# A two-layer strided convolution with a joint network: the first tap in two column parts, its load halves between the sample blocks, and every engine's order as a table

## The chip, the core and the metric

The kernel runs on one core of a Trainium2 chip. The metric is the device time of one execution, in microseconds (us). A core has five engines that each work through a queue of their own: TensorE (PE in the profile; its weight loads are PEld), VectorE (DVE), ScalarE (ACT), GpSimd (POOL) and SyncE (SP), which here only issues DMAs.

## What is computed

```python
def reference(x, w1, w2, g, w_f, w_g, w_o):      # x: (2, 4000, 512), w1, w2: (5, 512, 512), g: (2, 8, 512)
    pad = K // 2
    xp = jnp.pad(x, ((0,0),(pad,pad),(0,0)))
    h = sum over i of einsum("btc,cd->btd", xp[:, i:i+T, :], w1[i])
    h = _gelu(h)[:, ::2, :]
    ...
    f = _gelu(the same with hp and w2)[:, ::2, :]
    fe = jnp.einsum("btd,de->bte", f, w_f)
    ge = jnp.einsum("bud,de->bue", g, w_g)
    j = jnp.tanh(fe[:, :, None, :] + ge[:, None, :, :])
    return jnp.einsum("btud,dv->btuv", j, w_o)
```

Two convolutions of five taps over time, each followed by gelu and by keeping every second row, then for each of 2 x 8 pairs a tanh of a sum and a last product with w_o. All data is bf16; the output is (2, 1000, 8, 512).

## The kernel before

Everything lies transposed, channels in the 128 partitions (four blocks of 128 channels, k = 0 to 3), time along the columns. The program is first written down as a list of operations (class `Plan`), each with its engine, its reads and writes and a cost; `edges` finds what must wait for what, `schedule` sets the order of every engine, and `emit` writes the queues and semaphores. An operation made with `flex` may go to either of two engines, and `schedule` settles which.

The work comes in these stages.

- **Start.** A memset, eight products of zeros on PE (`warm_mm`), the loads on SP. The first 218 x 4 samples of batch 0 come as two blocks `xr[0]` (128 rows) and `xr[1]` (90 rows), each row four samples long. PE turns each block in two operations (even and odd sample phases, `pp` = 0 and 1) of eight transposes each, into PSUM banks 4 to 7; DVE copies the two results of the first block into `xs[0]` (line 527), ACT those of the second (line 525).
- **Direct products.** `direct(i, m)` multiplies tap i of w1, output block m, with columns of `xs[0]`: for the first 216 outputs of batch 0, two neighbouring outputs side by side (2 x 216 = 432 columns), four channel blocks each, into banks 0 to 3. The taps go in the order 0, 4, 2, 1, 3. Taps 0, 4 and 2 read even phases (2 and 0), taps 1 and 3 odd ones. Four ACT operations (line 712) apply gelu and write `hT[0]`.
- **Triples.** The rest of both layers goes by a scheme that makes three outputs from fewer products: `Triple` forms sums and differences of the samples (`step`, on DVE and ACT: "d", "r", "t2", "tm", "sm", "t1", "s1", ...), `w1part` and `w2part` form sums of the taps (on DVE and ACT, into `w1_t`, `w1_x`, `w2_t`), and `Unit` issues the products of one output block in five parts s1 to s5. The first two triples have 262 columns, the others 334.
- **Joint part.** `fe` and `ge`, then tanh on ACT into `jT` and `jX`, then the last product. It goes in blocks of four tiles by a scheme with seven products instead of eight (`Seven`: `sums` form operand sums, on POOL or DVE by `flex`; p1 to p7 are the products, whose results ACT or DVE evict and add), and some plain tiles (`Plain`). SP stores the tiles.

What sets the order around the change. On SP the order before is: `xr[0]`, `xr[1]`, tap 0 of w1 in two column halves (256 of 512 columns each, all four channel blocks), then taps 4, 2, 1, 3 whole, then twelve transposing loads into `xq`, six into `xp[2]`, and the rest. `load_w1` lets each whole tap wait for an earlier load (`o.after.append(came[-3].idx)`): tap 4 for `xr[0]`, tap 2 for `xr[1]`, tap 1 for tap 0, tap 3 for tap 4. In `schedule` a time line is played through with the costs; PE takes the earliest operation that is ready, SP and POOL by index, ACT and DVE by the latest time at which an operation may end, all but PE corrected by one letter for each operation in the string `NUDGES`. Operations made while `pl.pin` is set (all up to the gelu of the direct part) keep their order on their engine.

Of the kernel before, what the change touches and what calls it, by code (L numbers as in the profile page):

```python
# [12 lines left out]
P = 128  # L13
# [37 lines left out]
class Psum:  # L51
# [6 lines left out]
    def pair(self, lo, step, n):  # L58
        ap = self.h[:, lo:lo + 2 * step].rearrange("p (s c) -> p s c", s=2)[:, :, 0:n]
# [9 lines left out]
NUDGES = (  # L69
    "WWWWWWWWWWWWWWWWWWWWWWWWWWWWWWWWWWWWWWWWWWWWWWWWWWWWWWWWWWWWWWWWWWWWWWWWWWWWWWWZGRxV4s1q-S-zIwUDlPB1btjPJVWAWWfYOS-0KT0d"  # L70
    "dIkA-0yl2ZWWWWWWWWWWWyWWQEqWWMWWm8ddCa1B0-yn00WoWW2KtWW7WWPWWg8HCWeWW1mZWWDWW0WWakaF--VX-W0WWOrTWWXWWUWW5WwWWJ-4WW_WW-WW"
    "-5T00vmWGWW70RWW6WW-WWb-mtW4WWGlgWW0WW0WW6-a2YwvXTWiWWKSvWWsWWaWW0W-WW-n-WWcWW_WWjsHUAloWWWWWW5Jd-Pq-WBWWD-2WW4WWeWWw-S0"
    "0fmDvt3RUh-W-WWY--WW-WWAWWEX4iYejb0992kFIky15WNWW2tUWW6WWkWWfuUox0NRL-GW-WW_S8WWSWW4WW0-z4Oe-ByzWdWWh-eWWrWWXWWnLu0W0WWi"
    "8-WWHWWKWWBJ0VxX26uWSWWf1RWW-WWPWWTW-WWtS4WW1WWjWW9WWWW-Zk-d0WYWWq-pWWOWWWWWcO-AWNWW0pSWWQWWzWWPqIYZ---bW4WWi06WW-WW-WWl"
    "WWWWyWW46MD-WW7_0WlW0MW-W-eWZWwnW0Wb0WW_WWXWhWfWWrW-i0-S2VEu4WWsWWbWW0WW9qj9BWWqWW-WWWMe0z0WWoWWKWWWWW4WWsy092WWSWWWWWWL"
    "WWWWWZWW-WW-WWnWWSW0O-SrWWaWWZWWWHWWW8rzw6WWxWW-WWDWWkWWOwFlY6-WWPWWIWWWhWWWWWuoeb4WWYWWYWWiWWqWW7H3IDWWGWWIWWWsWW-n2WWy"
    "WWRWW0WW_WW9W4tRWWCWWLWWWEWWWWW00-X-WWpWWUWWxWWQWWjcm7aWW0WWqWWW-WWWGqTWWoWW-WWlWW-WFQ7DiWWEWWVWWW-WWWW00-g_sjWWUWW0WW-W"
    "W-WyN---WW-WW3WWWTWWc0zz-WWHWWwWWGWWsWp9TM-WWzWWLWWW0WWWyfWWDWW2WWAWWQWE7E0kWW-WWjWWW0WduWW0WWAWW4WWUWpxUpFWWlWW3WWWdWWW"
    "WWwWWOWWJWWLWlzPsiWWzWWoWWWyWg0EOWWqWWAWWqWW9E9XdWWNWW0WWWIWWWNG0-yKWWsWW8WWEWWbI0LPWW-WW6WWW0W1yWW8WWTWWhWWsI_qTWWqWWQW"
    "WWPWWWwBWW-WWrWW-WWpYyqiWWDWWZWWWUW49WW7WWdWWFWWp5_FFWWQWWWWWW6WWWdXE0WWLWWAWWrWW07LstWWWWWtWWWsWxEBY8cWW3WW1WWwWWOVPnsW"  # L80
    "W0WWJWWWOWWWGEWW0WWYWW-WWHCX_fWWmWWCWWW0WC4WWVWWFWWJWW0W-WW-j0WWrWWaWWWWW5WZ-WWfWWFWW1WWOWqW--rmWW5WWdWWWJWWWG-lSWWTWWPW"
    "WbWW0Rrw1WW-WWqWWWDWeXsFWW0WWpWWfWW82Id5WWkWWPWWW8WWW6EWWiWWYWWMWW7W1tSWWdWWkWWWeWx2WW3WW-WWMWWSUx45WWyWWYWWWFWWWWW3WWyW"
    "W-WWfWxWD-qzWW0WWJWWWcWWWTWWtWWrWWyWNWWWWzWWJWWW1WWUWW3WWXWWWhWW0WLWWiW")


class Plan:
# [88 lines left out]
    def schedule(self, pred):  # L175


        ops, HOP = self.ops, self.HOP
        n = len(ops)
        succ = [[] for _ in ops]  # L180
        for i, p in enumerate(pred):
            for j in p:
                succ[j].append(i)
        span = [o.cost + (4.0 if o.dma else 0.0) for o in ops]
        late, nextpe = [0.0] * n, 0.0
        for i in range(n - 1, -1, -1):
            t = min([late[s] - (HOP if pred[s][i] else ops[i].cost - span[i]) for s in succ[i]], default=0.0)
            if ops[i].eng == "pe":
                t = min(t, nextpe)
            late[i] = t - span[i]  # L190
            if ops[i].eng == "pe":
                nextpe = late[i]
        nudge = [0.1 * (ALPHABET.index(c) - 32) for c in NUDGES] if len(NUDGES) == n else [0.0] * n
        left = [len(p) for p in pred]
        ready = [0.0] * n
        free = {e: 0.75 for e in ("pe", "act", "dve", "pool", "sp")}
        cand = {e: [] for e in free}

        def engines(i):
            return ops[i].alt or (ops[i].eng,)  # L200

        for i in range(n):
            if not left[i]:
                for e in engines(i):
                    cand[e].append(i)
        order = {e: [] for e in free}
        wire, lock, start = 0.0, 0.0, [0.0] * n
        for _ in range(n):
            best = None
            for e, c in cand.items():  # L210
                if c:
                    t = max(free[e], min(ready[i] for i in c))
                    if best is None or t < best[0]:
                        best = (t, e)
            t, e = best
            now = [i for i in cand[e] if ready[i] <= t + 0.02]
            i = min(now, key=(lambda i: i) if e == "pe" else (lambda i: (0.15 * i + nudge[i], i)) if e in ("sp", "pool") else (lambda i: (late[i] + nudge[i], i)))
            for f in engines(i):
                cand[f].remove(i)
            order[e].append(i)  # L220
            o = ops[i]
            if o.alt:
                o.eng, (o.fn, o.cost), o.alt = e, o.alt[e], None
            start[i] = t
            free[e] = t + o.cost
            if o.port:
                if lock > t - 0.2 and e == "dve":
                    free[e] = max(t, lock) + o.cost + 0.2
                elif lock > t:
                    free[e] = lock + o.cost  # L230
                lock = free[e]
            end = free[e]
            if o.dma:
                wire = max(wire, t + 1.8) + o.wire
                end = max(wire, t + 2.0)
            for s in succ[i]:
                ready[s] = max(ready[s], end + HOP if pred[s][i] else free[e])
                left[s] -= 1
                if not left[s]:
                    for f in engines(s):  # L240
                        cand[f].append(s)
        self.start = start
        self.end = max(free.values())
        return order

    def emit(self, block, tail):
        nc, ops = self.nc, self.ops
        pred = self.edges()
        order = self.schedule(pred)
# [71 lines left out]
def bass_standalone__seq2seq_rnn_t_joint__speech_kernel(  # L321
# [25 lines left out]
    NA, N3 = 216, 262  # L347
# [9 lines left out]
    with ExitStack() as es:  # L357
# [33 lines left out]
        xq = [Buf(nc, f"xq{i}", [6, NK, 288], BF16, v.end - v.bytes) for i, v in enumerate((xs[1], w2_sb))]  # L391
# [85 lines left out]
        came = [load_xr(rt) for rt in range(2)]  # L477
        act(warm[0:1], warm[1:2], ACT.Gelu_apprx_tanh)

        def load_w1(i):  # L480
            src = w1[i].rearrange("(k c) d -> c k d", c=P)
            if len(came) == 2:
                h = D // 2
                for sl in (slice(0, h), slice(h, D)):
                    o = pl.dma("sp", lambda e, sl=sl: e.dma_start(w1_sb[i, :, sl].ap, src[:, :, sl]), (), (w1_sb[i, :, sl],), nbytes=262144)
            else:
                o = load_w("sp", w1_sb[i], src)
                o.after.append(came[-3].idx)
            came.append(o)

        def load_xq(i, ph):
            load_x6(xq[i], 0, ph, 2 * NA // 3 + i * N3 - 2, 0, -(-(N3 + 3 - i) // 16) * 16)

        for kind, i in (('w', 0), ('w', 4), ('w', 2), ('w', 1), ('w', 3), ('x', 4), ('x', 0), ('x', 2), ('x', 1), ('x', 3), ('x', 5)):
            if kind == "w":
                load_w1(i)
            else:
                load_xq(0, i)
        for ph in (4, 0, 2, 1, 3, 5):
            load_xq(1, ph)  # L500
# [8 lines left out]

        warm_mm(NWARM)  # L510
        psb = ps.h[:, :].bitcast(BF16)
        for rt in range(2):
            for pp in range(2):
                bk, n = 4 + 2 * pp + rt, NR[rt]
                pv = View(psb[:, bk * 1024:(bk + 1) * 1024].rearrange("p (r k c) -> p r k c", r=2, k=NK)[:, :, :, 0:n], np.array([bk]), True)

                def fn(e, rt=rt, pp=pp, pv=pv, n=n):
                    for r in range(2):
                        for k in range(NK):
                            ins = e.transpose(pv.ap[:, r, k, :], xr[rt].h[0:n, 2 * r + pp, k, :], ident.h[0:n, 0:n])  # L520
                    return ins
                pl.op("pe", fn, (xr[rt].rows(0, n), ident[:]), (pv,), 0.55)
                o = xs[0][pp::2, :, 16 + rt * P:16 + rt * P + n]
                if rt:
                    act(o, pv, ACT.Copy)
                else:
                    pl.op("dve", lambda e, o=o, pv=pv: e.tensor_copy(out=o.ap, in_=pv.ap), (pv,), (o,), vec_cost(o, (pv,)))
# [158 lines left out]
        for b in range(B):  # L686
            memset(hT[b][4:6, :, HOFF - 1:HOFF])
            memset(hT[b][:, :, HOFF + NT3:HOFF + NT3 + 2])
# [17 lines left out]
        for i in taps:  # L706
            for m in range(NK):
                direct(i, m)
# [437 lines left out]
```

## Time and profile before

| | us |
|---|---|
| median of 3 runs | 252.21 (251.29 to 252.4) |
| profiled execution | 252.07 |
| its span in the profile | 250.3 |
| around the span | 1.77 |
| PE busy in the span | 245.5 |
| DVE, ACT, POOL busy | 207.8, 209.9, 106.7 |
| first direct product starts | 7.29 |
| last product's result evicted by ACT from | 247.42 |

The clock granted to PE in the profiled execution is 1.00 of full speed. The profile gives the span of one execution, engine by engine. A line of the timeline gives start, duration, engine, source line, operation, the tile written and the tiles read, shapes and how many instructions are merged; in brackets the idle time before and what ended it. A busy time of PE is that of overlapping products and tells little of its pace; the distance between starts does.

### The profile page before, as it was taken

Reading aid. Unit: us, or ns where it says so; the run is one execution under the profiler, and the core shown is the slowest. Engines: PE = TensorE matmul, PEld = TensorE weight load, DVE = VectorE, ACT = ScalarE, POOL = GpSimd, SP = SyncE. Lnnn points to the kernel's source line nnn. Section 1 sums busy time; section 2 is a strip of 40 time slices with the busy share of each in tenths; the row PEclk is TensorE's granted clock in tenths of the full one; section 3 lists DMA queues with packets and bytes.
Section 4 is the critical chain, followed back from the end, with each engine's and each line's share of the span. In section 5 each row is a group of like instructions: output and inputs, shape, how many; then the busy total and the mean of one; then the engine's idle time right before and its main releaser. Section 6 shows DMA issues by size and latency. Waiting matters only on the chain.

```text
span 250.3 us, 5204 instructions
## 1 busy us (share of the span) xinstructions
PE 245.5 (98%) x1920; PEld 184.5 (74%) x1920; DVE 207.8 (83%) x346; ACT 209.9 (84%) x354; POOL 106.7 (43%) x109
## 2 busy tenths in 40 slices
PE   8999999999999999999999999999999999999995
PEld 4556888887666666667467878877778888888873
DVE  1599999968999997981528978899899999999763
ACT  2297799978969868963699998999999999999673
POOL 1000000000000000002429898598998999998910
PEclk9999999999999999999999999999999999999999
DMA  7999999988500052000002223422344444564547
GB/s 212 307 187 173 192 164 212 147 173 262 163 0 3 0 169 85 1 1 3 0 0 84 86 84 105 151 88 84 112 145 131 160 154 141 171 211 156 185 162 240
DMA packets 57392, 31.92 MB, mean 128 GB/s; under 512 B 33837, under 2 KB 57149, under 8 KB 57367
## 3 DMA queue, kind: packets, MB, share of 16 engines
q1 hardware_dynamic: 57367, 31.59, 48.2%
q8 instruction: 15, 0.25, 0.4%
q14 instruction: 10, 0.08, 0.1%
HBM read 7.71 MB, written 16.38 MB: 96 GB/s over the span
## 4 chain that ended last, share of the span: by engine, by line
PE 89%; DVE 4%; DMA 4%; ACT 1%; issue 1%; DVEq 0%
PE acc L442 89%; DMA w_sb<-in_w_dram 2%; DMA xr<-in_x_dram 1%; DVE ssum L429 1%; DVE ssum L530 1%; DVE w_t L429 1%; DVE row L429 1%; ACT hT L434 1%; ACT w_x L434 0%; ACT ost L434 0%; DVE w_x L429 0%; ACT sd L434 0%; DVEq L282 0%
## 5 line engine op out<-in xcount | busy, mean ns | idle before, releaser
L429 DVE TENSOR_TENSOR og<-acc,sn 128x512 bf16<-128x512 f32 x87 | 56.7, 680 | 5.4 <-PE acc L442 4.7
L434 ACT ACTIVATE jT<-feT,geT 128x1000 bf16<-128x1000 f32 (+6 forms) x56 | 51.3, 961 | 0.5 <-DVE feT L755 0.4
L442 PE MATMUL acc<-tw,ss 128*128 128x256 f16 x348 | 48.3, 273 | 0.0
L442 PEld LDWEIGHTS acc<-tw,ss 128*128 128x128 f16 x348 | 33.7, 98 | 7.0 <-issue 0.4
L931 POOL TENSOR_TENSOR ss<-jT 128x512 f16<-128x512 bf16 x26 | 31.4, 1218 | 11.8 <-ACT jT L434 9.2
L442 PE MATMUL acc<-row,w_sb 128*128 128x334 bf16 (+1 forms) x192 | 33.1, 295 | 0.0
L862 ACT ACTIVATE sn<-acc 128x512 f32<-128x512 f32 x51 | 30.6, 619 | 2.6 <-PE acc L442 2.3
L442 PE MATMUL acc<-wo_sb,jT 128*128 128x256 bf16 (+1 forms) x196 | 31.6, 288 | 0.0
L426 POOL MEMSET hT<- 128x8 bf16 (+2 forms) x6 | 0.7, 149 | 71.6 <-ACT hT L434 66.7
L442 PE MATMUL acc<-row,w_x 128*128 128x262 bf16 (+1 forms) x192 | 28.5, 290 | 0.2 <-ACT sd L434 0.2
L434 ACT ACTIVATE jX<-feT,geT 128x1000 bf16<-128x1000 f32 (+4 forms) x28 | 25.0, 919 | 0.0
L442 PEld LDWEIGHTS acc<-row,w_sb 128*128 128x128 bf16 x192 | 18.5, 98 | 6.7 <-DVE acc L530 0.3
L442 PEld LDWEIGHTS acc<-row,w_x 128*128 128x128 bf16 x192 | 18.6, 98 | 6.1 <-ACT sd L434 0.5
L442 PEld LDWEIGHTS acc<-wo_sb,jT 128*128 128x128 bf16 x196 | 19.1, 98 | 5.3
L434 ACT ACTIVATE sd<-acc 128x334 f32<-128x334 f32 (+1 forms) x48 | 20.3, 429 | 2.6 <-PE acc L442 2.1
L530 DVE SCALAR_TENSOR_TENSOR acc<-acc,sd 128x334 f32<-128x334 f32 (+1 forms) x24 | 11.6, 482 | 11.4 <-PE acc L442 11.4
L434 ACT ACTIVATE hT<-acc 128x262 bf16<-128x262 f32 (+2 forms) x36 | 15.4, 433 | 6.7 <-PE acc L442 6.6
L863 DVE COPY sn<-acc 128x512 f32<-128x512 f32 x26 | 17.6, 682 | 3.9 <-PE acc L442 3.9
L931 POOL TENSOR_TENSOR ss<-jX 128x512 f16<-128x512 bf16 x17 | 20.3, 1209 | 1.2 <-ACT jX L434 0.7
L931 POOL TENSOR_TENSOR ss<-jT,ss 128x512 f16<-128x512 bf16 x15 | 17.8, 1191 | 1.0 <-DVE ss L931 0.7
L442 PE MATMUL acc<-wo_sb,ss 128*128 128x256 bf16 x116 | 17.7, 273 | 0.0
L931 POOL TENSOR_TENSOR ss<-ss,jT 128x512 f16<-128x512 f16 x15 | 17.5, 1173 | 0.6 <-DVE ss L931 0.4
(105 smaller groups left out, 499.7 us busy)
## 6 DMA issues: line engine op xcount, KB each, us to landing
out_dram<-og SPq DMA_DIRECT2D x44, 256.0 KB, 2.2
w_sb<-in_w_dram SPq DMA_DIRECT2D x9, 512.0 KB, 5.1
out_dram<-og SPq DMA_DIRECT2D x14, 128.0 KB, 2.2
out_dram<-ost SPq DMA_DIRECT2D x7, 128.0 KB, 2.0
xr<-in_x_dram SPq DMA_DIRECT2D x1, 512.0 KB, 3.4
w_sb<-in_w_dram SPq DMA_DIRECT2D x2, 256.0 KB, 5.3
wf_sb<-in_w_f_dram SPq DMA_DIRECT2D x1, 512.0 KB, 3.7
wg_sb<-in_w_g_dram SPq DMA_DIRECT2D x1, 512.0 KB, 4.7
```

Of the source, the lines that this page charges most:

```text
L426: pl.op("pool", lambda e: e.memset(v.ap, 0.0), (), (v,))
L429: pl.op(eng, lambda e: e.tensor_tensor(out=o.ap, in0=a.ap, in1=b.ap, op=op), (a, b), (o,), 0.02 + 2.14e-3 * o.ap.free_size() if eng == "po ...
L434: pl.op("act", lambda e: e.activation(o.ap, i.ap, func, scale=scale, bias=0.0 if bias is None else bias.ap), rd, (o,), o.ap.free_size() * ...
L442: ins = e.matmul(o.ap, lhsT=l.ap, rhs=r.ap, start=start and n == 0, stop=stop and n == len(pairs) - 1, skip_group_check=not check)
L530: pl.op(eng, lambda e: e.scalar_tensor_tensor(out=o.ap, in0=a.ap, scalar=f, in1=b.ap, op0=ALU.mult, op1=add), (a, b), (o,), vec_cost(o, (a ...
L862: pl.flex({"act": (lambda e: e.activation(o.ap, v.ap, ACT.Copy), 0.05 + n * 0.833e-3), "dve": (lambda e: e.tensor_copy(out=o.ap, in_=v.ap) ...
L863: "dve": (lambda e: e.tensor_copy(out=o.ap, in_=v.ap), 0.065 + n * 1.04e-3)}, (v,), (o,))
L931: fn = lambda e, o=S[i], x=x, y=y, op=op: e.tensor_tensor(out=o.ap, in0=x.ap, in1=y.ap, op=op)
```

## The change

1. **Loads.** Tap 0 of w1 is loaded in halves by channel block (k = 0, 1 and k = 2, 3, all 512 columns) instead of by output column. The order on SP becomes `xr[0]`, first half, `xr[1]`, second half, tap 4, 2, 1, 3. Tap 4 waits for no earlier load any more; tap 2 waits for `xr[1]`, tap 1 for tap 0's second half, tap 3 for tap 4.
2. **Tap 0 in two column parts.** The outputs 0 to 127 of each of the two halves (2 x 128 = 256 columns) need only the first block; they are multiplied first, for k = 0, 1 and then for k = 2, 3. Then the outputs 128 to 215 (2 x 88 = 176 columns). Instead of 16 products of 432 columns there are 16 of 256 and 16 of 176.
3. **The second block's turn** goes behind the first eight products of tap 0.
4. **Copies.** Of each block, DVE copies the even phases and ACT the odd ones.
5. **Order.** `schedule` no longer plans: `ORDER` gives the indices of all 1643 operations (12 more than before) engine by engine, two letters for each. For `flex` operations the table settles the engine, too. DVE has 369 operations (346 before), ACT 343 (353), POOL 92 (105), SP 142 (142), PE 697 (685). SP's order behind the first eight loads is the one of before.
6. `N3` becomes a pair with the same two values, and the width of `xq` is worked out from it to the same 288. `pair` writes its access pattern so that the second part may lie across the end of the first pair. The memsets of `hT` and `xq` change place in the list.

```diff
+ORDER = {
+    "pe": (
+        "0X0Y0Z0a0b0c0d0e0f0h0l0m0n0o0p0r0t0u0v0w0x0y0z0_0-101112131415161718191A1B1C1D1E1F1G2O1s1H1I352o1u1v2V2W2Q2R2q2y2z2r"
...
+    def schedule(self):
+
+        order = {k: [64 * ALPHABET.index(a) + ALPHABET.index(b) for a, b in zip(s[::2], s[1::2])] for k, s in ORDER.items()}
+        assert sorted(i for v in order.values() for i in v) == list(range(len(self.ops)))
+        for k, v in order.items():
+            for i in v:
+                o = self.ops[i]
+                if o.alt:
+                    o.eng, (o.fn, o.cost), o.alt = k, o.alt[k], None
...
-        came = [load_xr(rt) for rt in range(2)]
+        def load_w1(i, parts=1, ks=(0,)):
+            n = NK // parts
+            for k in ks:
+                src = w1[i, k * P:(k + n) * P].rearrange("(k c) d -> c k d", c=P)
+                dst = w1_sb[i, k:k + n]
+                o = pl.dma("sp", lambda e, dst=dst, src=src: e.dma_start(dst.ap, src), (), (dst,), nbytes=n * 131072)
+                if len(came) > 4:
+                    o.after.append(came[-3].idx)
+                came.append(o)
+
+        came = [load_xr(0)]
+        load_w1(0, 2, (0,))
+        came.append(load_xr(1))
+        load_w1(0, 2, (2,))
         act(warm[0:1], warm[1:2], ACT.Gelu_apprx_tanh)
...
+        load_w1(4)
+        for i in (2, 1, 3):
+            load_w1(i)
...
         warm_mm(NWARM)
...
+        turn(0, 0, "dve")
+        turn(0, 1, "act")
...
+        for q0, n in ((0, P), (P, NA - P)):
+            for ks in ((0, 1), (2, 3)):
+                for m in range(NK):
+                    mm(ps.pair(m * NT + q0, NA, n), [(w1_sb[0, k, m * P:(m + 1) * P], both(0, k, q0, n)) for k in ks],
+                       q0 == 0 and ks[0] == 0, False, False)
+                if q0 == 0 and ks[0] == 0:
+                    turn(1, 0, "dve")
+                    turn(1, 1, "act")
+        for i in taps[1:]:
+            for m in range(NK):
+                direct(i, m)
```

`turn(rt, pp, eng)` holds the eight transposes of one block's phases and the copy of their result, as the loop at lines 512 to 527 did, with the engine of the copy as an argument.

More of the change, by code (lines that the diff above doesn't have):

```diff
@@ L58, in pair @@
     def pair(self, lo, step, n):
[L59 removed]
+        lo_ap = self.h[:, lo:lo + n]
+        ap = bass.AP(tensor=lo_ap.tensor, offset=lo_ap.offset, ap=[list(lo_ap.ap[0]), [step, 2], [1, n]])
         cells = np.unique(np.concatenate([np.arange(lo, lo + n), np.arange(lo + step, lo + step + n)]) // 512)
@@ L173, in edges @@
         return pred
[L175 to L243, printed above, removed]
@@ L247, in emit @@
         nc, ops = self.nc, self.ops
-        pred = self.edges()
-        order = self.schedule(pred)
+        order = self.schedule()
         pred = self.edges()
@@ L390, in bass_standalone__seq2seq_rnn_t_joint__speech_kernel @@
         assert all(xp[i].end <= xs[i].end for i in xp)
-        xq = [Buf(nc, f"xq{i}", [6, NK, 288], BF16, v.end - v.bytes) for i, v in enumerate((xs[1], w2_sb))]
+        XQ = [-(-(N3[i] + 3 - i) // 16) * 16 for i in range(2)]
+        xq = [Buf(nc, f"xq{i}", [6, NK, XQ[i] + 16], BF16, v.end - v.bytes) for i, v in enumerate((xs[1], w2_sb))]
         assert xq[0].end <= xs[1].end and xq[1].end <= w2_sb.end
```

137 lines of the change are left out of this document (70 added, 67 removed).

## The prediction

> **What bounds the kernel now.** I read the page's engine shares first, then the chain of work that ended last, the timeline of the first 30 us, and the busy time by stretches.
>
> ```profile
> PE 245.5 (98%) x1920; PEld 184.5 (74%) x1920; DVE 207.8 (83%) x346; ACT 209.9 (84%) x354; POOL 106.7 (43%) x109
> ```
>
> PE is busy almost throughout. A busy PE need not be at its pace, so I compared start-to-start distances of the products with the pace of their width: 0.183 us for 432 columns (80 products, 14.81 us, below), 0.112 for 262, 0.109 for 256. From the first product at 7.29 to the last, all the waits together are about 0.9 us.
>
> ```profile
> 4.58 2.17 PE L520 MATMUL acc<-ident,xr 128*128 128x128 bf16 x32
> ...
> 5.67 1.29 DVE L527 COPY xs<-acc 128x1024 bf16<-128x1024 bf16 x2 [4.54 <-PE acc L520]
> 6.46 1.44 ACT L434 ACTIVATE xs<-acc 128x720 bf16<-128x720 bf16 x2 [4.23 <-PE acc L520]
> ...
> 7.29 14.81 PE L442 MATMUL acc<-xs,w_sb 128*128 128x432 bf16 x80 [0.54 <-ACT xs L434]
> 9.77 1.29 DVE L530 SCALAR_TENSOR_TENSOR ssum<-w_sb 128x512 f32<-128x512 bf16 x2 [2.81 <-DMA w_sb<-in_w_dram]
> ...
> 21.94 1.50 PE L442 MATMUL acc<-row,w_x 128*128 128x262 bf16 x12
> ...
> 23.61 2.99 PE L442 MATMUL acc<-row,w_x 128*128 128x262 bf16 x24 [0.17 <-ACT sd L434]
> ```
>
> Columns are start, duration, engine. All 32 turns of the sample blocks come first, two copies on DVE and two on ACT follow, and the first product starts when ACT's first copy (6.46 to 7.23) is done. The waits: 21.94 + 12 x 0.112 = 23.28, but the next product starts at 23.61 (0.33); another 0.12 before 25.08; 0.10 in two small ones up to 32; and 0.36 from 34 us on, of which 0.15 at 136.9 and 0.13 at 238.5.
>
> ```profile
> 0.74 3.45 DMA xr<-in_x_dram
> 4.18 0.02 issue
> 4.20 5.55 DMA w_sb<-in_w_dram
> 9.75 0.02 issue
> 9.77 1.29 DVE ssum L530 x2
> ...
> 23.61 223.79 PE acc L442 x1788
> ```
>
> This is the chain in order of time. Before 23.61 it does not run through PE: it runs from the landing of tap 4 of w1 (9.75) through DVE, which has no pause from there:
>
> ```profile
> 9.77:23.60 13.83, 13.67 (x80) 7.54 (x78) 13.83 (x23) 10.35 (x17) 0.24 (x2) 1.00 1.02 204
> 23.60:34.00 10.40, 10.39 (x91) 8.59 (x92) 10.40 (x21) 7.90 (x17) 0.33 (x2) 1.00 1.09 188
> ...
> 125.00:180.00 55.00, 55.00 (x436) 42.27 (x435) 45.24 (x75) 54.34 (x86) 43.80 (x38) 1.00 0.27 87
> 180.00:240.00 60.00, 60.00 (x528) 50.82 (x526) 55.83 (x91) 57.23 (x93) 56.43 (x49) 1.00 0.49 159
> ```
>
> After length and sum stand PE, PEld, DVE, ACT, POOL (instructions in brackets), clock, DMA. DVE is full in both early stretches. So two things must come earlier for the end to move: PE's first product, and DVE's results.
>
> **The start.** Nothing changes until the first block is turned: it lands at 4.18, 16 transposes follow from 4.58, DVE's copy runs 5.67 to 6.36. The first piece of tap 0 needs this copy and half of w1's tap 0, which now travels second. Half a tap is 262 KB, 0.74 us at the 354 GB/s below, so it lands near 5; 1.3 us to spare. With 0.06 from a copy's end to a product (7.23 to 7.29 above), products start at 6.42 instead of 7.29: 0.87 earlier. But the second block's 16 transposes (starts 5.93 to 6.54 at 0.039 apart, 0.64 with the last) stood before 7.29 where PE would have waited anyway; now they stand between products and cost 0.64. The pieces of tap 0: 16 of 256 columns at 0.109, and 16 of 176 columns, between the 90-column (0.039) and 256-column rows, on the line through 262 and 432 columns 0.076. Together 2.96 against 16 x 0.183 = 2.93: 0.03 lost (-0.4 if free, +0.5 at the 256-column row). Net 0.87 - 0.64 - 0.03 = **0.20 earlier**. Cover: the second block landed at 5.67; 0.74 later at most is 6.4, and its transposes start at 6.42 + 8 x 0.109 = 7.29. Its DVE copy (0.5) ends near 8.3, wanted at 8.80. Tap 0's other half, at worst 7.6 as now, is wanted at 7.93.
>
> Two copies (first block's odd rows, second block's odd rows) go on ACT behind two w_x conversions that wait for DVE's chain. They run about 13.4 to 15.1 (conversions 12.30 to 13.5 now, copies 1.03 and 0.77) and are wanted by tap 1 at 6.42 + 0.64 + 2.96 + 5.86 = 15.88: hidden, 0.8 of cover. POOL now has an xp memset that waits for the last direct product (22 us) ahead of the memsets of hT and xq; their readers come after 30 us, and the xq ones wait for a load landing at 33 anyway. SP's queue keeps its order behind the start, so its stores cost nothing new.
>
> **DVE's chain.** It starts when tap 4 lands. Tap 4 no longer waits for the first block on SP (issue 4.20), but that wait hides nothing: the DMA engines are full, in rows of the stretches:
>
> ```profile
> 5.00:6.50 1.50, 1.50 (x29) 1.50 (x27) 0.83 (x2) 0.04 (x1) 0.00 (x0) 1.00 1.14 279
> 7.50:10.50 3.00, 3.00 (x18) 1.63 (x17) 0.73 (x2) 0.39 (x1) 0.00 (x0) 1.00 1.06 354
> ```
>
> The first holds tap 0's column halves (packets of 512 bytes), the second whole taps (1024 bytes). The new halves are row blocks with 1024-byte packets: 524 KB at 354 instead of 279 GB/s take 1.48 instead of 1.88 us, so all that follows, tap 4 first, lands about **0.4 earlier**: 9.35. Bounds: 0, and 1.2 (tap 4's 5.55 us behind an issue at about 3.0 is 8.55).
>
> The Trainium skill, page DMA: Bandwidth & Descriptors, section Specifications, gives 512 bytes as the least transfer for line rate; by that rule the old halves already ran at it and tap 4 would come no sooner. The two rows above disagree with it, 279 against 354, though the first stretch also holds other packets. This is the third rival below.
>
> Now DVE's new queue. In the order before, the step "t1" of the first triple, which PE's third group of products (s3) reads, is the 24th DVE instruction from 9.77 and starts at 23.71, 0.606 apiece. In the table it is the 27th: three more weight sums of later column blocks stand ahead. It starts at 9.35 + 26 x 0.606 = 25.11, and is there for PE at 25.11 + 0.70 + 0.06 = 25.87. PE reaches s3 after 6.42 + 0.64 + 2.96 + 64 x 0.183 + 32 x 0.112 = 25.31. So a new wait of **0.56** before s3 takes the place of 0.33 and 0.12; 0.10 of small ones stay. Lateness of PE at 34 us: after 6.42 + 0.64 + 0.03 + 0.56 + 0.10 = 7.75; before 7.29 + 0.33 + 0.12 + 0.10 = 7.84. The start's 0.20 comes out as **0.09**: DVE eats the rest. If tap 4 comes as now it is 0.31 worse, +0.3 in all; if it comes 1.2 earlier PE never waits and 0.7 is won.
>
> **The table behind 34 us.** Matching indices (the new program has 12 more, all in the start), 27 strided sums leave POOL for DVE and 14 go back: net 13. Net 10 evictions and copies leave ACT for DVE.
>
> ```profile
> L931 POOL TENSOR_TENSOR ss<-jT x26: 1147/1164/1397, 130.0 to 235.3; 128x512 f16<-128x512 bf16 x26
> ...
> L931 DVE TENSOR_TENSOR ss<-jT x11: 412/426/907, 125.9 to 232.8; 128x512 f16<-128x512 bf16 x11
> ...
> L931 DVE TENSOR_TENSOR ss<-ss,jT x4: 424/1313/1357, 129.4 to 164.2; 128x512 f16<-128x512 f16 x4
> ```
>
> Minimum, median, maximum in ns: a sum on DVE takes 0.42, but up to 1.36 where one on POOL is running. DVE gets 13 x 0.42 + 10 x 0.60 = 11.5 us at best, while the 30 sums already there (mean 0.70) may lose up to 30 x 0.28 = 8.4 as POOL gets 13 fewer. I wrote out the table's queues with these durations: each instruction starts when its engine and its inputs allow. No product waits over 0.1 except one: near 238.5 a p4 product needs the eviction of p7, which stands on DVE behind a sum that meets a POOL sum or just misses it: 0.43 or 0. All waits behind 34 us: 0.11 to 0.54, against 0.36 now; I take the middle, 0.33, **0.03 won** (bounds -0.25 and +0.2; below these lies only the second rival).
>
> **The sum.** 0.09 + 0.03 = 0.1 us off the profiled execution, whose time is 252.07 (span 250.3 and 1.77 around it): 251.95. The median shown is 252.21, 0.14 above; I give **251.9**. 0.5%, 1.26 us, is about what a measurement of this kernel can tell from no change.
>
> **Rivals.**
> 1. Tap 4 lands 0.8 to 1.2 earlier, as its issue is earlier and its packets need not follow the others. Then the wait before s3 is 0.2 or none, and without the wait at 238.5: 0.7 + 0.25, 251.1. For it: 2.81 us of DVE idle before 9.77; against: DMA shares over 1. Chance 0.17; a third of it lies beyond 0.5%.
> 2. Slower: DVE becomes the bound. If all sums on DVE stay at a mean of 0.70, it gets 13 x 0.70 + 10 x 0.60 = 15.1 us in the stretches 125 to 240, where it has 9.8 + 4.2 = 14.0 idle; the spare is never all usable, so +1.1 and some: 253.6. It decides from (14.0 - 6.0) / 13 = 0.62 us a sum upward. For it: 56 of 60 us busy in the second stretch; against: POOL's load falls by 13 x 1.16 = 15 us. Chance 0.10.
> 3. Packet size changes nothing and tap 4 lands at 9.75: 252.07 + 0.3 = 252.3. Chance 0.15.
> 4. The change doesn't do what it says, because a piece waits for its load, or PE's clock falls in the pause from 5.93 to 6.42. The pause of 0.7 before 7.29 now left the clock at 1.00. DVE's queue hides up to 0.56 of such a loss: 252.0 to 252.5. Chance 0.08.
>
> The forecast itself, 251.5 to 252.4, has 0.50. Faster by over 0.5% 0.07, slower by over 0.5% 0.10, the rest, 0.83, within. The range takes in rivals 1, 3 and 4 and the doubt of a median (the three times shown span 1.1): 251.0 to 252.9.
>
> **What will show it.** First product of 256 columns at 6.4 and 16 transposes of 90 behind the eighth; DVE's first weight sum at 9.35; a wait of some 0.56 before s3 near 25.9, released by DVE; ACT's two copies near 14 without a wait of PE; sums on DVE mostly at 0.42. Wrong would make it: a wait at 7.3 or 7.9 released by a load, a PE wait for ACT near 15.9, or many sums on DVE over 1 us with PE waiting behind them.

## The result and the profile after

The changed kernel takes **254.09 us** (median of 4 runs, 253.67 to 254.34) where the kernel before takes 252.12 (4 runs, 251.29 to 252.4). The ratio is 1.0085, with a 95% interval of 1.0068 to 1.0101: slower by about 2 us. The forecast was 251.9, with a range up to 252.9. The profiled execution took 254.12, with a span of 252.3 against 250.3. Two executions at a granted clock of 0.974 (265.04 of the kernel before, 266.29 in experiment 7) are in no median or ratio of this text.

The page's engine shares, first as before:

```profile
PE 245.6 (97%) x1932; PEld 186.2 (74%) x1936; DVE 212.8 (84%) x369; ACT 203.6 (81%) x344; POOL 90.0 (36%) x96
```

The work has moved as the diff says (POOL 106.7 to 90.0, ACT 209.9 to 203.6, DVE 207.8 to 212.8), and PE's is the same (the page lacks the records of four of the 1936 products that the change should show). So the 2 us are waits and a longer end. The timeline of the start:

```profile
4.57 1.91 PE L485 MATMUL acc<-ident,xr 128*128 128x128 bf16 x16
...
6.42 1.24 PE L407 MATMUL acc<-xs,w_sb 128*128 128x256 bf16 x8
...
7.50 0.81 PE L485 MATMUL acc<-ident,xr 90*128 90x90 bf16 x16
...
9.18 0.69 DVE L499 SCALAR_TENSOR_TENSOR ssum<-w_sb 128x512 f32<-128x512 bf16 x1 [0.62 <-DMA w_sb<-in_w_dram]
```

The first product starts at 6.42, as forecast, and the first weight sum at 9.18 (forecast 9.35). The chain in order of time shows where the execution then waited:

```profile
9.58 7.47 DMA xq<-in_x_dram
17.07 1.08 ACT row L399
...
24.14 0.29 ACT sd L399
24.42 0.05 issue
24.47 96.84 PE acc L407 x748
...
133.21 1.91 DVE ss L908 x2
135.12 0.61 DVE og L394
135.73 0.05 issue
135.78 83.10 PE acc L407 x700
...
248.56 0.38 ACT ost L399
```

The early part runs no longer through DVE from tap 4 on, but through the first load into `xq` and ACT. A second piece that was not there before leads through ACT and DVE to 135.78; its last steps are two sums on DVE and the `og` behind them. The stretches:

```profile
5.00:6.50 1.50, 1.50 (x15) 1.30 (x14) 0.69 (x1) 0.00 (x0) 0.00 (x0) 1.00 0.96 275
7.50:10.50 3.00, 3.00 (x44) 2.82 (x42) 1.86 (x4) 0.00 (x0) 0.00 (x0) 1.00 0.80 242
...
125.00:180.00 55.00, 53.95 (x425) 41.37 (x425) 47.21 (x87) 51.50 (x81) 35.15 (x31) 1.00 0.26 85
180.00:240.00 60.00, 59.90 (x525) 50.76 (x525) 57.45 (x102) 55.99 (x88) 50.89 (x46) 1.00 0.48 157
```

The DMA engines, full from 7.5 to 10.5 before (354 GB/s), moved 242. From 5.0 to 6.5 they moved 275, no more than the 279 of before.

To add the waits up I use PE's **lateness**: the start of a product, less what all products ahead of it take at the pace of their width (the start-to-start distances of each width, as in the prediction; a product without a record is counted in where the gap shows it). It rises only where PE waits. The last column is what follows the last product.

| us | at 9 | at 34 | at 132 | at 136.5 | at the end | to the span's end |
|---|---|---|---|---|---|---|
| before | 7.30 | 7.87 | 7.88 | 7.88 | 8.34 | 3.07 |
| after | 7.28 | 8.05 | 8.16 | 9.33 | 9.44 | 3.98 |
| start alone | 6.94 | 8.49 | 8.50 | 8.51 | 8.96 | 3.07 |
| table alone | 7.85 | 7.87 | 7.98 | 9.15 | 9.26 | 3.72 |
| after, w_o sums first | 7.10 | 7.85 | 7.96 | 7.97 | 8.08 | 3.72 |
| the same, more ACT instructions | 7.10 | 8.14 | 8.47 | 8.47 | 8.58 | 3.17 |

The first two rows give the loss of the profiled execution: 0.18 up to 34 us, 0.10 from there to 132, 1.17 at 135.8, less 0.35 that is saved behind it, and 0.91 in the tail; 0.03 more is tap 0 in pieces. The other rows are experiments.

### The profile page after: what moved, and what is told of

Same layout as the page of the kernel before. It is cut to its first block, busy times and chain, and to the rows that moved or that the text cites. A ratio compares the mean times of both kernels' runs of the same rounds, so it can differ in the third digit from the quotient of the medians.

```text
span 252.3 us, 5204 instructions
## 1 busy us (share of the span) xinstructions
PE 245.6 (97%) x1932; PEld 186.2 (74%) x1936; DVE 212.8 (84%) x369; ACT 203.6 (81%) x344; POOL 90.0 (36%) x96
## 4 chain that ended last, share of the span: by engine, by line
PE 83%; ACT 6%; DMA 6%; DVE 3%; SPq 1%; issue 1%; ACTq 0%
PE acc L407 83%; DMA xq<-in_x_dram 3%; DMA w_sb<-in_w_dram 3%; ACT jT L399 2%; DVE ss L908 1%; ACT row L399 1%; ACT feT L399 1%; ACT w_x L399 1%; ACT hT L399 0%; DVE ost L840 0%; DVE sn L840 0%; SPq L447 0%; ACT w_t L399 0%; SPq L433 0%; DVE og L394 0%
## 5 line engine op out<-in xcount | busy, mean ns | idle before, releaser
L407 PE MATMUL acc<-tw,ss 128*128 128x256 f16 x348 | 55.2, 273 | 0.0
L407 PE MATMUL acc<-wo_sb,jT 128*128 128x256 bf16 (+1 forms) x192 | 34.3, 286 | 1.2 <-DVE og L394 1.0
L908 POOL TENSOR_TENSOR ss<-jT 128x512 f16<-128x512 bf16 x20 | 23.0, 1163 | 32.0 <-DVE feT L732 24.6
L407 PE MATMUL acc<-row,w_sb 128*128 128x334 bf16 (+1 forms) x192 | 31.6, 295 | 0.0
L839 ACT ACTIVATE sn<-acc 128x512 f32<-128x512 f32 x46 | 26.9, 601 | 5.8 <-PE acc L407 5.7
L840 DVE COPY sn<-acc 128x512 f32<-128x512 f32 x31 | 20.8, 682 | 1.0 <-PE acc L407 0.9
L407 PE MATMUL acc<-wo_sb,ss 128*128 128x256 bf16 x116 | 21.0, 273 | 0.0
L908 POOL TENSOR_TENSOR ss<-jT,ss 128x512 f16<-128x512 bf16 x14 | 16.6, 1190 | 4.9 <-DVE ss L908 4.6
L407 PE MATMUL acc<-row,w_t 128*128 128x334 bf16 x96 | 16.9, 305 | 0.0
L407 PE MATMUL acc<-hT,w_sb 128*128 128x334 bf16 x96 | 16.8, 305 | 0.0
```

The costliest lines, as they stand in the source:

```text
L407: ins = e.matmul(o.ap, lhsT=l.ap, rhs=r.ap, start=start and n == 0, stop=stop and n == len(pairs) - 1, skip_group_check=not check)
L839: pl.flex({"act": (lambda e: e.activation(o.ap, v.ap, ACT.Copy), 0.05 + n * 0.833e-3), "dve": (lambda e: e.tensor_copy(out=o.ap, in_=v.ap) ...
L840: "dve": (lambda e: e.tensor_copy(out=o.ap, in_=v.ap), 0.065 + n * 1.04e-3)}, (v,), (o,))
L908: fn = lambda e, o=S[i], x=x, y=y, op=op: e.tensor_tensor(out=o.ap, in0=x.ap, in1=y.ap, op=op)
```

## The experiments

All ratios are to the kernel before, measured on the same chip; intervals are 95%. In the first three expectations the letters stand for theories: A lays the loss on the table behind 34 us, above all on the order of POOL's sums, and holds the start for nearly free; B lays it on too many sums on DVE everywhere, C on the start, and each text gives its numbers.

**1. The start alone, and the table alone.** The first has the changed program with the order of before on all engines behind the start. The second has the program before, with the changed kernel's order behind the start written as a table. In both, only the table and `schedule` differ from the kernel that they are made from.

```diff
-        order = self.schedule(pred)
+        order = self.schedule()
```

> The change at the start alone (loads, tap 0 in two parts, the second turn amid its products, its copies), with every engine's order behind it as before, indices moved by 12. Theory A: the start is worth between 0.3 us less and 0.3 us more, ratio 0.999 to 1.001, no wait of PE over 0.3 us from 34 us on. Rival C (the start makes PE and DVE late and upsets what follows): ratio 1.005 or more.

> The start as before the change, the table's order behind it, indices moved back by 12. Theory A: the wait of 1.2 us near 135.8 and the longer end are there, the time is 1.5 to 2.2 us over the kernel before, ratio 1.006 to 1.009. Rival C: ratio below 1.003.

Start alone: 252.75, ratio 1.0039 (1.0027 to 1.0052). Table alone: 253.36, ratio 1.0062 (1.0049 to 1.0075). **Both parts lose**, 1.0 and 1.6 us; together that is more than the 2.0 of the change, so the two losses do not simply add up. Theory A was right on the table. On the start both theories missed: 1.0039 lies above A's range (to 1.001) and below C's (from 1.005).

**2. The w_o sums first.** Four sums over w_o (`wosums`, 1.2 us each, they need nothing but a load) stand on POOL. The table puts the first operand sum of the joint part ahead of them, which needs a tanh. POOL in the changed kernel:

```profile
127.23 1.16 POOL L908 TENSOR_TENSOR ss<-jT 128x512 f16<-128x512 bf16 x1 [24.60 <-DVE feT L732]
128.35 2.45 POOL L394 TENSOR_TENSOR tw<-wo_sb 128x512 f16<-128x512 bf16 x2
131.16 1.27 POOL L908 TENSOR_TENSOR ss<-jT,ss 128x512 f16<-128x512 bf16 x1 [0.36 <-DVE ss L908]
132.39 2.45 POOL L394 TENSOR_TENSOR tw<-wo_sb,tw 128x512 f16<-128x512 bf16 x2
```

and in the kernel before:

```profile
117.12 2.26 POOL L429 TENSOR_TENSOR tw<-wo_sb 128x512 f16<-128x512 bf16 x2 [16.71 <-PE acc L442]
119.34 2.40 POOL L429 TENSOR_TENSOR tw<-wo_sb,tw 128x512 f16<-128x512 bf16 x2
```

POOL idles 24.6 us and then does the four at the time when DVE has its first sums. DVE there, changed kernel:

```profile
133.13 1.99 DVE L908 TENSOR_TENSOR ss<-jT 128x512 f16<-128x512 bf16 x2
135.04 0.68 DVE L394 TENSOR_TENSOR og<-acc,sn 128x512 bf16<-128x512 f32 x1
```

Two sums, 0.75 us when alone (below), take 1.99. They run beside POOL's last pair (132.39 to 134.84): the first ends at 133.82 and the second at 135.12, each 0.28 behind the end of one sum of the pair (133.54 and 134.84). PE waits for the `og` behind them. The experiment moves one entry of the table:

```diff
-        "010203042C050j0k1J2D1K1L1M5q8YAP9i9kAQ9j9lCNCPBmCOBpC-DYD1D0E9EgEhDZE8EAFHFsEiGMGLGqGNGsGrHIHnHJIpJIHKHLJlHoIMHpIKIL"
+        "010203042C050j0k1J2D1K1L1M5q8Y9i9k9j9lAPAQCNCPBmCOBpC-DYD1D0E9EgEhDZE8EAFHFsEiGMGLGqGNGsGrHIHnHJIpJIHKHLJlHoIMHpIKILIn"
```

> The changed kernel with one edit: on POOL the four sums of w_o (tw) stand again ahead of the first two operand sums (ss), as before the change. Theory A (the loss is the wait of 1.2 us near 135.8: a first ss sum placed ahead of the tw sums holds them until 127, and two ss sums on DVE then run into them and take 2.0 us instead of 0.8): the tw sums end before 123, the wait of PE near 135 is gone, the time is 1.0 to 1.4 us under that of the change, about 252.9 against 254.1, ratio to the kernel before about 1.003. Rival B (DVE has too many sums everywhere): the wait stays or moves, the time stays within 0.4 us of 254.1. Either way the 0.9 us that the end took more (from the last product to the end of the span) is open.

252.88, ratio 1.0044 (1.0029 to 1.0060): 1.0 us better than the change, as A had it. The w_o sums ended at 127.03, later than the 123 of the text and early enough. DVE at the same place:

```profile
132.90 0.75 DVE L907 TENSOR_TENSOR ss<-jT 128x512 f16<-128x512 bf16 x2
133.57 0.68 DVE L393 TENSOR_TENSOR og<-acc,sn 128x512 bf16<-128x512 f32 x1
```

The sums are back at 0.75 and the wait of 1.16 is gone (lateness 7.96 at 132, 7.97 at 136.5). This cause is shown.

**3. More instructions on ACT.** In all kernels with the table, "w_o sums first" among them, the span ends 0.6 or more later behind the last product. In that run SP issues the last store 0.72 behind the last product as before, but it lands 2.58 us after its issue instead of 1.93. What differs in the queues is a packet of the program itself. The "w_o sums first" run from 247 us on (the last column is us from issue to landing):

```profile
q14 instruction: 1, 0.01, 0.3%
...
out_dram<-ost SPq DMA_DIRECT2D x1, 64.0 KB, 2.6
```

and the kernel before, which has no instruction packet there:

```profile
out_dram<-ost SPq DMA_DIRECT2D x1, 64.0 KB, 1.9
```

Four of the ten packets on this queue come, with either order, when ACT has some 64, 190, 317 and 448 recorded instructions behind it, four when DVE has 63, 188, 316 and 446. The table takes ten evictions from ACT, so ACT's last packet moves from 238.7 to 249.0 (250.7 in the changed kernel). In all four kernels with the table and without the edit below, the last store lands 1.14 behind the start of this packet.

```diff
-        act(warm[0:1], warm[1:2], ACT.Gelu_apprx_tanh)
+        def prime(e):
+            for i in range(24):
+                ins = e.activation(warm[2 + i:3 + i].ap, warm[1:2].ap, ACT.Gelu_apprx_tanh, scale=1.0, bias=0.0)
+            return ins
+        pl.op("act", prime, (warm[1:2],), (warm[2:26],), 0.2)
```

> The kernel with the four w_o sums ahead of the operand sum on POOL (1.0044 of before), with 24 one-element activations on ACT near 2 us in place of one. In all kernels with the new table an instruction packet of 8 KB is read 1.14 us before the last store lands (250.67 and 251.81 in the changed kernel), and the last store takes 2.57 us from issue to landing; with the order of before ACT's packet is read at 238.7 and the last store takes 1.93. In both orders it comes when ACT has some 447 instructions behind it. Fetch theory: ACT lost instructions to DVE, so its last fetch now falls behind the last stores and delays them; with 23 more ACT instructions in front it is read before 247, the last store lands 1.9 to 2.1 after its issue, 0.6 less, and the ratio is 1.001 to 1.003. Backlog theory: the late landing is due to SP's queue of stores and the packet only stands beside it; then the last store still takes 2.5 or more and the ratio stays at 1.004 to 1.005.

252.26, ratio 1.0021 (1.0007 to 1.0036). The packet is read at 237.8, no instruction packet is left behind 247, and the last store:

```profile
out_dram<-ost SPq DMA_DIRECT2D x1, 64.0 KB, 2.0
```

lands 2.01 after its issue. **23 useless instructions won 0.6 us.** The intervals of the two ratios overlap; the tail shows it more directly, 3.17 instead of 3.72. The backlog theory falls for this part.

**4. Tap 4 waits again.** Does tap 4 land 0.6 earlier (9.15 against 9.75) because it is issued earlier, or because of the loads ahead of it?

```diff
         load_w1(4)
+        came[-1].after.append(came[0].idx)
```

> The changed kernel, but tap 4 of w1 waits for the first sample block on SP again, as before the change. If tap 4 comes earlier (9.15 instead of 9.75) because of the larger packets of tap 0, it still lands by 9.3; if because of its earlier issue, it lands at 9.6 or later. The time is no part of the question: 253.7 to 254.4.

Issued at 4.17 instead of 2.63, tap 4 landed at 9.18 instead of 9.15 (one execution, 254.03 us). The earlier issue is worth nothing here. That leaves the other loads, and not the packets of tap 0 alone: the four loads ahead of tap 4 were in at 7.81 in the changed kernel, later than the 7.58 of before. Tap 2, which travels beside tap 4, is issued at 7.23 there and at 5.68 before. With tap 2 issued at 4.88 (the first run of experiment 5) tap 4 landed at 9.33, with the start alone at 9.02. How much each is worth is not separated.

**5. The start: which wait?** DVE and PE with the start alone:

```profile
15.86 0.69 DVE L392 TENSOR_TENSOR w_x<-w_sb 128x1024 bf16<-128x1024 bf16 x1 [1.01 <-DMA w_sb<-in_w_dram]
```

```profile
24.27 2.99 PE L405 MATMUL acc<-row,w_x 128*128 128x262 bf16 x24 [1.15 <-ACT sd L397]
```

DVE waits 1.01 for tap 3, which lands at 15.83 instead of 14.52. Two candidates: the loads, or ACT's copies at 13.0 to 14.7 that delay its `sd`. The first run lets tap 2 no longer wait for the second sample block, which in the changed order lands at 6.9 to 7.4 instead of 5.6:

```diff
-                    o.after.append(came[-3].idx)
+                    o.after.append(came[1 if len(came) == 5 else -3].idx)
```

> This is the kernel with the start alone changed (1.0039 of before), with one edit: the load of tap 2 is held until the first half of tap 0 has landed (4.8 us) and no longer until the second sample block has (7.1). Loads theory: the start loses because the second sample block lands 1.5 us later than in before (7.10 against 5.67); tap 2 is held for it, so the DMA engines have little to do from 8 to 9 us (106 GB/s against 352), and tap 3 and the first xq load come late (15.83 and 16.80 against 14.52 and 15.59); DVE waited 1.01 us for tap 3. Then here the stretch 8 to 9 runs above 300 GB/s, tap 3 lands before 14.8, DVE's wait for it is under 0.3, PE's wait near 24.3 falls from 1.31 to 0.6 or less, and the ratio is 0.999 to 1.002. Copies theory: the start loses because ACT makes its two copies from 13.0 to 14.7, amid the conversions that DVE's and PE's triples wait for. Then the wait near 24.3 stays at 1.0 or more and the ratio at 1.003 to 1.005.

252.34, ratio 1.0026 (1.0012 to 1.0040). The hole from 8 to 9 us closed (357 GB/s), taps 2 and 1 came 0.3 earlier, but tap 3 still landed at 15.87, and PE lost 1.11 near 24 (1.31 with the start alone, from start to start). By this wait the run spoke for the copies, and its ratio lies between the two theories' ranges; what it shows is that the held load is not what delays tap 3. The second run puts ACT's two copies first in its queue (the beginning of ACT's row of the table):

```diff
-        "0A1X1Z0i0s1R1_
+        "0A0i0s1X1Z1R1_
```

> The kernel with the start alone changed, with one edit: ACT's two copies of the sample blocks stand ahead of the first two w_x conversions, so that they run near 6 and 8 us, where ACT is idle. Copies theory: PE's wait near 24.3 falls from 1.31 to 0.6 or less, ratio 0.999 to 1.002. Loads theory: DVE still waits about 1 us for tap 3 near 15.8, the wait near 24.3 stays at 1.0 or more, ratio 1.003 to 1.005.

252.47, ratio 1.0023 (1.0012 to 1.0035). PE lost 0.69 near 24. DVE:

```profile
15.29 0.69 DVE L392 TENSOR_TENSOR w_x<-w_sb 128x1024 bf16<-128x1024 bf16 x1 [0.45 <-DMA w_sb<-in_w_dram]
```

This looks like a half win for the copies, but in this execution tap 3 landed earlier, at 15.26. The runs of this study with the order of before, in which DVE waits for tap 3 (the last two rows are runs of experiment 6), settle it:

| | tap 3 lands | PE goes on | difference |
|---|---|---|---|
| start alone | 15.83 | 24.27 | 8.44 |
| tap 2 not held | 15.87 | 24.30 | 8.43 |
| copies early | 15.26 | 23.70 | 8.44 |
| start alone, 32 warm-up products | 15.84 | 24.27 | 8.43 |
| before, 24 warm-up products | 16.09 | 24.52 | 8.43 |

Whatever ACT does, PE goes on 8.43 or 8.44 after tap 3's landing. **In this wait the copies cost nothing; the landing sets it.** Why tap 3 landed 0.6 earlier with the copies early is not shown by one execution of each. With the new table three more weight sums hide tap 3, and the first `xq` load takes its place: it lands at 17.05, 16.57, 16.53 and 16.96 in the four runs with table and start, and PE goes on 7.42, 7.48, 7.43 and 7.60 later.

**6. Why do tap 3 and the first `xq` load land late?** In every run the DMA engines all but stand still between 12.5 and 18 us: 16 to 21 packets of the first transposing loads, 0.02 us each as a rule, take far longer, the longest of each run 1.1 to 2.6 us. DMA share and GB/s by microsecond, before:

```profile
14.00:15.00 1.00, 1.00 (x8) 0.50 (x6) 1.00 (x3) 1.00 (x3) 0.00 (x0) 1.00 0.96 204
15.00:16.00 1.00, 1.00 (x7) 0.58 (x6) 1.00 (x3) 1.00 (x3) 0.00 (x0) 1.00 1.28 258
16.00:17.00 1.00, 1.00 (x7) 0.49 (x5) 1.00 (x2) 1.00 (x2) 0.00 (x0) 1.00 1.26 105
17.00:18.00 1.00, 1.00 (x7) 0.57 (x6) 1.00 (x3) 0.72 (x2) 0.00 (x0) 1.00 0.75 97
```

and with the start alone:

```profile
14.00:15.00 1.00, 1.00 (x7) 0.53 (x6) 0.85 (x2) 1.00 (x3) 0.00 (x0) 1.00 2.21 60
15.00:16.00 1.00, 1.00 (x8) 0.54 (x6) 0.14 (x1) 1.00 (x2) 0.00 (x0) 1.00 0.29 58
16.00:17.00 1.00, 1.00 (x7) 0.54 (x6) 1.00 (x2) 1.00 (x3) 0.00 (x0) 1.00 1.28 287
```

Before, the long stall (16.5 to 17.8) comes when tap 3 and the first `xq` load are in; with the start alone (14.3 to 15.9) both still wait behind it, and tap 3 lands as it ends. A 16 KB packet of PE's own program, which comes at 80 to 95 products (warm-up products and transposes counted), starts 0.6 and 0.9 ahead of it (15.91 and 13.39), and the change puts 16 more products ahead. So I suspected the packet, and tried it from both sides, by cutting the warm-up products into narrower ones: 24 instructions more for the start alone, 16 more for the kernel before.

```diff
-                mm(o, [(z, zz)], True, True)
-                pl.ops[-1].cost = 0.43
+                def fn(e):
+                    a = 0
+                    for w in (256, 128, 128):
+                        ins = e.matmul(o.ap[:, a:a + w], lhsT=z.ap, rhs=zz.ap[:, a:a + w], start=True, stop=True)
+                        a += w
+                    return ins
+                pl.op("pe", fn, (z, zz), (o,), 0.43)
```

(For the start alone and the two kernels below, four of 128 columns.)

> The kernel with the start alone changed (1.0039 of before), with 32 warm-up products of 128 columns in place of 8 of 512: the same columns, 24 instructions more for PE. Fetch theory of the start: PE's program is read in packets of 16 KB, one of which comes when PE has done 80 to 95 products; the change puts 16 more products ahead, so it comes at 11.9 to 14.3 us instead of 15.1 to 15.9, and there it meets the first transposing loads: 20 of their packets then take 1.4 to 2.5 us each and nothing else moves, so tap 3 and the first xq load land late (15.83 and 16.80 against 14.52 and 15.59). With 24 more products in front the packet comes at 8 to 10.5 us, where only plain loads are under way: tap 3 lands by 14.6, xq's first load by 15.7, DVE's wait for tap 3 (1.01) is under 0.3, PE's wait near 24.3 is 0.7 or less, ratio 0.998 to 1.001. If the packet only stands beside the stall (the transposing loads stall by themselves), tap 3 lands at 15.3 or later and the ratio stays at 1.003 to 1.005.

> The kernel before, with 24 warm-up products (8 of 256 and 16 of 128 columns) in place of 8 of 512: 16 instructions more for PE, as many as the change puts ahead, and nothing else. Fetch theory of the start: PE's packet comes at 12 to 14 us instead of 15.1 to 15.9, ten or more transposing packets take over 1.2 us there, tap 3 and the first xq load land 0.7 us later or more (over 15.2 or over 16.3), and the ratio is 1.001 to 1.004, without any other part of the change. Otherwise: landings as in before (14.52, 15.59), ratio 0.999 to 1.001.

Start alone: 252.69, ratio 1.0029 (1.0019 to 1.0040). The packet came at 12.31, earlier but not as early as I had worked out, and the stall stayed (13.7 to 15.6, tap 3 at 15.84): a packet ahead of the transposing loads does not spare them. Kernel before: the packet came at 12.82 and the stall at 13.3 to 15.9, with nothing but the warm-up products changed:

```profile
13.00:14.00 1.00, 1.00 (x7) 0.56 (x6) 1.00 (x3) 1.00 (x2) 0.00 (x0) 1.00 3.52 167
14.00:15.00 1.00, 1.00 (x8) 0.51 (x6) 1.00 (x2) 1.00 (x3) 0.00 (x0) 1.00 0.07 15
15.00:16.00 1.00, 1.00 (x7) 0.57 (x6) 0.17 (x1) 0.84 (x1) 0.00 (x0) 1.00 0.24 57
```

Tap 3 landed at 16.09 and PE waited 0.88 at 24.5. This execution took 252.98, the slowest of its twelve; their median, 251.99, is a ratio of 1.0012 (0.9999 to 1.0026). So the long stall fell early here with instructions alone added, in the direction of the change. But ten of the twelve executions took 252.3 or less, so how often it does is not settled.

Nor is the packet's part. In all fourteen profiles a first stall starts 0.45 to 0.50 behind the first transposing packet, wherever PE's packet is. In nine of them, in which PE's packet came before it or 0.2 behind its start, this is the long one (longest packet 1.5 to 2.6 us); the kernel before with 24 warm-up products is one of them. In the other five (before, the change, start alone, table alone, second block second) it ends after 0.5 to 0.9, and the long one (1.1 to 1.5) follows 0.4 to 0.9 behind PE's packet. So the transposing loads stall without PE's packet; whether the packet sets the second stall or the length is open.

**7. The second block second.** What is left of the change when the load that comes late goes back to its place, with its turn ahead of all products and ACT's copies early (parts of SP's and PE's rows of the table; ACT's as above):

```diff
-        "06070809
+        "06080709
...
-0f0h0l0m0n0o0p0r
+0f0h0p0r0l0m0n0o
```

> The kernel with the start alone changed, with the second sample block loaded second again (as in before), its transposes ahead of all products, and ACT's copies near 6 and 7 us. What is left of the change is tap 0 in two row halves of 1024-byte packets and in two column parts. Loads theory: the second block lands at 5.6 to 5.8, the first product starts at 6.6 to 6.9, the first half of tap 0 lands near 6.5, tap 3 before 14.6, and PE's wait near 24 is 0.4 or less. If the packet size makes the loads faster, as the prediction held, tap 4 lands at 9.2 to 9.4 and the ratio is 0.996 to 1.000; if it does nothing, tap 4 lands at 9.6 to 9.8 as in before (9.75) and the ratio is 0.999 to 1.002.

252.08, ratio 1.0019 (0.9999 to 1.0040). The second block lands at 5.59, tap 4 at 8.56 (earlier than either case of the text, and at the early bound of the prediction, 8.55), tap 3 at 13.60. The first product starts only at 7.30, later than the text had it: PE still ran at half its later pace up to 7.1. PE has no wait near 24; it has one of 0.25 at 35.6 and one of 0.14 at 46 instead, behind later loads. With 32 narrow warm-up products, which bring the packet to 10.7 and the first `xq` load to 15.13 (16.04 without), both a little later than the text asks:

> The kernel with the second sample block loaded second and the copies early (1.0019), with 32 warm-up products of 128 columns. Fetch theory of the start: the packet comes at 8 to 10.5, the first xq load lands by 15 (16.04 without), PE's waits up to 50 us, 0.39 without, are under 0.2, ratio 0.995 to 0.999, a version faster than before. Otherwise 1.000 to 1.003.

251.59, ratio **0.9989** (0.9979 to 0.9999), lateness 7.19 at 34 us and 7.65 at the end:

```profile
21.89 4.18 PE L405 MATMUL acc<-row,w_x 128*128 128x262 bf16 x36
```

36 products where before there were 12 and then a wait. It is the best version that I found, by 0.3 us, less than this measurement can tell from no change by the bound of the prediction. Last, the changed kernel with all of this, the w_o sums first and the ACT instructions:

> The changed kernel with everything mended that the runs named: the w_o sums ahead on POOL, the second block loaded and turned second, ACT's copies early, 24 small activations more on ACT, 32 narrow warm-up products. If these are all the causes, nothing is left of the loss and the start's and the table's gains show: ratio 0.994 to 0.999. If a cause is missing, 1.001 or more.

251.83, ratio 1.0008 (0.9989 to 1.0026), between the two cases of the text. Its profiled execution is good (251.20, span 249.4, lateness 7.43 at the end, 0.9 less than before). The 0.9 is there at 9 us already (6.38 against 7.30): PE's pace doubled at 4.2 in this execution and at 5.5 in that of before. That goes with no edit (6.0 and 6.9 in the other two runs with 32 warm-up products), so the good time is in part luck. Its twelve runs spread from 251.03 to 253.24, where the kernel before spans 251.22 to 252.44. What comes and goes there is open.

## Why the prediction was wrong, step by step

- **The step that failed most is "The table behind 34 us"**, with its "All waits behind 34 us: 0.11 to 0.54". They came to 1.39 (lateness 8.05 to 9.44). The prediction shows and counts the operand sums alone as what can hold DVE. The w_o sums, sums on POOL too, stand nowhere in it, and the table puts an operand sum ahead of them that must wait for a tanh. One wait of 1.16 stood there; moving one entry took it away (experiment 2). The second rival's 253.6 is near the result for the wrong reason: it let the mean of DVE's sums stay at 0.70, and over all 43 it fell to 0.46, as the forecast had it. One sum was slow (1.37), one other took 0.78:

```profile
L908 POOL TENSOR_TENSOR ss<-jT x20: 1145/1156/1337, 127.2 to 239.8; 128x512 f16<-128x512 bf16 x20
L908 DVE TENSOR_TENSOR ss<-jT x17: 408/417/1371, 129.2 to 238.4; 128x512 f16<-128x512 bf16 x17
```

- **"SP's queue keeps its order behind the start, so its stores cost nothing new"** failed by 0.91 in the profiled execution. Of this 0.64 goes with the program packet of ACT (experiment 3). The other 0.27 is that SP issued the last store 0.99 behind the last product and not 0.72: from 246.07 on it issues seven stores nearly without a pause and comes to the last at 249.24, 0.29 after ACT's eviction for it has ended (248.95).
- **"The start": right in its first event, wrong in what follows and in its worth.** The first product started at 6.42. The second block, "0.74 later at most", landed 1.54 later, at 7.21. The working gave every product its later pace; in this execution the transposes were 0.107 apart and the first products 0.213, and only from 6.95 on 0.109, so lateness at 9 us was 7.28 and not 7.09. An earlier doubling is no cure: in "w_o sums first" the first product started at 5.80, PE then waited 0.62 for the second block, and lateness was 7.10; in the start alone it was 6.94. The start hardly counts anyway: with the table alone lateness was 7.85 at 9 us and 7.87 at 34, as with 7.30 before. What counts near 24 us is when loads land.
- **ACT's copies "hidden, 0.8 of cover"**: right. They ran from 13.11 to 14.78, and PE has no wait near 15.9.
- **Packets: right in kind, wrong for "all that follows".** With the block second, where besides the form of the halves only tap 4's issue moves, both halves need 1.50, 1.48 and 1.45 us behind the second block (three runs), the column halves 1.91, 1.88 and 1.69 (before, table alone, before with 24 warm-up products). The stretch that moved 279 GB/s before moves 341 there:

```profile
5.00:6.50 1.50, 1.50 (x17) 1.50 (x16) 0.69 (x1) 0.00 (x0) 0.00 (x0) 1.00 1.06 341
```

  The Trainium skill, page DMA: Bandwidth & Descriptors, section Specifications, puts line rate at 512 bytes already; these rows disagree with it. In the changed kernel the place of the second block takes the gain back (275 GB/s, both halves in at 7.81). Tap 4 landed at 9.15, forecast 9.35, but not by the forecast's path alone (experiment 4), so this agreement is in part luck. Tap 3 landed at 14.56 as before (14.52) and the first `xq` load at 17.05 instead of 15.59: no 0.4 reached the loads that DVE and ACT wait for.
- **DVE's chain: right in itself, and it missed the wait ahead of it.** DVE's "t1" was forecast for 25.11 and started at 25.20. But PE had lost 0.72 at 24.47 to ACT, behind the late `xq` load, a wait that the prediction has nowhere, and came to s3 only at 26.27, when "t1" was done. The size of the two waits agrees (0.56 and 0.72) by luck. Where the first wait was only 0.36, in the run of experiment 4, PE waited a second time, 0.52 up to 26.28, about where the forecast had it.
- **The wait near 238.5**, "0.43 or 0": it was not there.

Together: about 1.0 for the w_o sums and 0.6 for the packet, of the 2.0 that the change loses. The 0.5 that is left in experiment 3 is not taken apart by a run; in its profile PE is 0.27 later than before at 34 us, behind the late `xq` load.

## What to carry to other kernels

An order written as a table is as good as its worst place: go through every instruction that slows one on another engine (here the sums on POOL and DVE), not only those of the kind that the change moves, and look where an engine that idled for long (POOL, 24.6 us) now starts late. In a stage that is bound by loads, follow each load to the consumer that waits last; a first product that starts 0.9 earlier is worth nothing if a load four places on lands no earlier. And count instructions: here the program of PE, ACT and DVE came in packets on DMA queues, and ten instructions fewer or 23 more on ACT moved one of them by 10 and 11 us.

## What the hardware did that was not expected

- A program packet of 8 KB beside the last store went with a landing 2.54 to 2.58 us after issue in the four profiles with the table and without the extra ACT instructions, against 1.91 to 2.01 in the ten profiles where the packet came earlier. The Trainium skill, page Runtime: NRT & Kernel Launch, section Instruction fetch mechanics, calls the cost of crossing a 16 KiB boundary of an engine's program mostly hidden; what shows here is another cost, of a store beside such a packet.
- The first transposing loads stall 0.45 to 0.50 us behind their first packet in all fourteen profiles, in five of them for 0.5 to 0.9 us and once more later, in nine at once for 1.5 to 2.6 us, in the longest with nearly nothing else moving on the DMA engines. Later loads stall near PE's next packet (32.0; 32.7 to 34.0 in the changed kernel). What sets the stalls off stays open.
- PE's pace doubled anywhere from 3.8 to 7.1 us in the profiles of this case, with warm-up products that started at 1.19 in all of them and a granted clock of 1.00 in the rows.
